# A fused long convolution and gated FFN: x rows loaded singly, index work on GpSimd, and the 1174 steps in a new order

## The chip, the cores and the metric

The kernel runs on one core of a Trainium2 chip. The metric is the device time of one execution in microseconds, the median of several runs. Engines are named as in the profile: PE (TensorE, matmuls), DVE (VectorE), ACT (ScalarE), POOL (GpSimd), and SP (SyncE), which here only issues DMAs. Each engine runs its own instructions strictly in order and waits on semaphores for the others.

## The reference

x, k and v are 2048 x 640 (S x D), all bfloat16; F is 1728. The layer norm of x feeds two branches, and the second gates the result:

```python
xn = layernorm(x)
# branch A: a 4-tap causal shift of k, times v, then a long causal convolution
kv = sum(k_pad[:, t:t+S, :] * shift_k[:, 3-t] for t in range(4)) * v
y  = irfft(rfft(kv, 2*S) * rfft(ssm_k, 2*S))[:S] + kv * ssm_D
s  = xn * y
# branch B: feed-forward
g  = silu(gelu(xn @ w1 + b1) @ w2 + b2)
out = x + s * g
```

## The kernel before

**The convolution** is done with matmuls. A transform of 4096 points is taken in two stages. Stage one multiplies with 128x128 matrices WA and WB, which are sines that the kernel makes itself from integer products of row and column numbers; stage two multiplies with 32x32 matrices `mats`, also made on the chip. Between the stages the rows have to change places, so stage one's result goes to DRAM (scrU for kv, scrK for the convolution's own kernel ssm_k) and comes back in another order. The two spectra are multiplied on DVE, taken back through 32x32 blocks (`ma`, `mb`), stored to scrC, loaded, and taken through stage one's inverse (`y`).

**Steps.** A hand-written `prologue()` opens the kernel: x chunk 0 (four rows of 128 partitions x 640) is loaded and normed, turned around on PE into xnT, and the first six blocks of the first FFN matmul are made. It also loads the small parameters: the taps skp, and b1 and ssm_D into one tile prm (`load_params`, three loads on ACT's queue), which PE turns around at L750. Then a string PLAN of 1174 steps is run in its order; each step issues one or a few instructions, and the string is the only thing that sets the order on each engine. The steps that matter below:

- `cv` (L534, L541, L545): kv on DVE, 128x1280 each: 64 steps in eight slices of eight; in each slice four products with a tap and three sums (L545, L541), and last the product with v (L534). cv31 finishes slice 3, cv63 slice 7, and `uf` 6i to 6i+5 read slice i
- `kf`, `uf` (L501): stage one for ssm_k and for kv; `ke`, `ue` move the result out of PSUM; `ks`, `us` store it (L516, L527), `fl`, `ml` load it again
- `ff`, `mu` (stage two) and `ma`, `mb` (its inverse): `blocks()`, four matmuls 32x32 (L395)
- `mp`, `mq` (L605): the products of a `mu` result in PSUM with the kernel's spectrum and its swapped copy, which `ma` and `mb` read; `me` moves their sum out of PSUM
- `h`, `he`, `g`, `ge` (L440, L447, L461, L467): FFN matmuls, gelu, FFN matmuls, silu
- `ls`, `lv`, `lr`, `ln`, `tt`, `te`: layer norm of x chunks 1 to 3 and their turning
- `w` (L299, the AND of the 128x2048 integer table) and `s` (the small matrices' integer table), which sines on ACT (`ws`, `ss`) then read

A mark .a or .d behind a step that moves data out of PSUM, or norms a row, says whether ACT or DVE does it (`evac`, L140). The block matmuls put their four 32x32 pieces at a quarter of the array that depends on the step's number:

```python
def blocks(out, m, rhs, turn, start=True, stop=True):
    for i in range(P // QB):
        j = (i + turn) % (P // QB)
        a, b = (slice(x * QB, (x + 1) * QB) for x in ((i, j) if m == F2 else (j, i)))
        nc.tensor.matmul(out=out[b, :], lhsT=mats[a, m, a], rhs=rhs[a, :], start=start, stop=stop)
```

`turn` is the step's number, P // QB is 4. The calls `ff`, `mu` of equal number modulo 4 use the same four pieces, and so do `ma` and `mb`, with the sign of the shift the other way.

Tiles, buffers and semaphores are handled by the framework. DMAs that SP and ACT issue signal one of eight completion semaphores, DMAHW0 to DMAHW7, given out in turn over the program; GpSimd's have eight of their own.

Of the kernel before, what the change touches and what calls it, by code (L numbers as in the profile page):

```python
# [28 lines left out]
WARM = (6, 3, 1)  # L29
# [3 lines left out]
w em4 em7 X1 he1 he0 he2 he3 ls6 ls7 ls5 K1 B0 h10 K0 B1 C4 he4 ls4 B2 ee7.a ee4.a he5 cv16 em6 ee6.a he10 h6 he6 lv1  # L33
lr1 ln6.a ln5.a ln4.a h13 h9 em5 he13 ee5.a h8 h11 he8 he9 s h12 he11 cv0 cv17 ln7.a cv8 he12 cv1 cv9 cv18 cv19 cv2 h7
tt8 tt9 tt7 tt6 cv20 cv10 cv11 te9.d he7 g0 g1 g2 C0 C1 C3 te6.d cv21 ws0 C2 ge0 te8.d cv22 cv3 ws1 d ge1 ge2 kt15
kc15.a kt7 cv12 te7.d kc7.d kt13 kt6 kt0 kt14 kc13.d V2 K2 kt1 kt5 kt8 kc0.d kc6.d tt5 kt2 kt11 kc14.d ws2 kc5.d V7
te5.d kc11.d kc1.a kt9 kf47 kc9.d kf46 kc8.a ke46.a kt3 kc3.a kt12 kc2.d kt4 kf28 kt10 K3 kc12.d kc4.d kc10.d cv13
gm0.d ke47.a kf40 ke40.a ke28.a kf4 kf17 kf29 kf26 kf16 ke17.a ke29.a ke26.a kf15 kf10 ke16.a ke10.a ke4.a g3 cv4 cv23
cv5 kf39 ge3 ke15.d gm1.d ke39.a kf41 kf34 kf5 ke5.a kf11 X2 kf45 kf27 kf33 ke11.a kf3 ke45.a ke3.a cv14 gm2.d cv40
gm3.d cv41 V0 X3 cv6 V1 g4 ke34.a ke33.a ke27.a ke41.a ks5 kf24 kf21 ke24.a kf14 kf44 kf42 kf7 kf43 cv42 cv15 ge4  # L40
ke44.a ke14.a ke42.a ke21.a ke7.a g5 ks1 ks9 ks13 kf12 kf8 kf25 kf20 ke43.d ls10 cv32 cv7 ge5 cv33 gm4.d kf0 ke12.a
# [46 lines left out]
def kernel(  # L88
# [139 lines left out]
    def load_x(c):  # L228
        for h in range(1 if c else 2):
            js = slice(2 * h, CH if c else 2 * h + 2)  # L230
            nc.sync.dma_start(out=xn_tiles[c][:, js, :], in_=x_v[:, c * CH:(c + 1) * CH, :][:, js, :])
# [439 lines left out]
    def prologue():  # L671
# [51 lines left out]
        for i in range(3):  # L723
            load_w1(i)
# [114 lines left out]
```

## Time and profile before

| | |
|---|---|
| median of 3 runs | 202.29 us (202.22 to 202.81) |
| profiled execution | 202.03 us, span 200.2 us |
| granted PE clock | 0.997 |
| PE, DVE, ACT, POOL busy | 95%, 86%, 77%, 22% of the span |
| data moved | 57.7 MB, mean 288 GB/s |
| first block matmul (L717) | 8.57 us |
| last kv product (cv31) ends | 84.43 us |

Times are in microseconds from the span's start. A timeline row has start, length, engine, line, operation, output and inputs, and in brackets how long the engine was idle before it and what the profile names as the end of that. A row "DVE L143 CAST ... x5" stands for five instructions in a row. ACTq and SPq are the queues that issue DMAs, PEld is the loading of PE's weights.

### The profile page before, as it was taken

The numbers are of one execution on the slowest core, as the hardware profiler recorded it, in microseconds if no ns is written. First come the engines' busy times: TensorE is split into PE (matmuls) and PEld (weight loads), VectorE is DVE, ScalarE is ACT, GpSimd is POOL, SyncE is SP. The second block draws the span as 40 slices with busy tenths as digits, with TensorE's granted clock in tenths as the row PEclk, the third lists the DMA queues.
The fourth block names the chain that finished last, engine by engine and source line by source line (L and its number), as shares of the span: only waits on it lengthen the run. The fifth ranks groups of instructions, "written<-read, shape, count | busy, mean of one in ns | idle before, by whom it ended". The sixth has DMA issues, their size and how long they took to land.

```text
span 200.2 us, 5094 instructions
## 1 busy us (share of the span) xinstructions
PE 191.1 (95%) x1934; PEld 111.4 (56%) x1934; DVE 172.8 (86%) x370; ACT 154.3 (77%) x303; POOL 45.0 (22%) x78
## 2 busy tenths in 40 slices
PE   7799999999999999999989999999999999999990
PEld 2484468866654545664645433347665454667760
DVE  7889999999999999999988999999999300199991
ACT  3469999999999999999979999984868557611030
POOL 8202000013475622153030001011055700001230
PEclk9999999999999999999999999999999999999998
DMA  6999999377699499999699999979368869991373
GB/s 196 354 394 331 361 391 411 124 263 265 184 399 419 151 328 328 363 390 384 234 276 366 337 313 315 298 271 284 92 209 291 307 185 338 395 393 52 134 273 123
DMA packets 27055, 57.69 MB, mean 288 GB/s; under 512 B 3030, under 2 KB 15511, under 8 KB 27030
## 3 DMA queue, kind: packets, MB, share of 16 engines
q1 hardware_dynamic: 22528, 39.65, 58.5%
q0 software_dynamic: 4320, 17.70, 23.5%
q8 instruction: 15, 0.25, 0.5%
q14 instruction: 10, 0.08, 0.1%
q10 hardware_dynamic: 182, 0.01, 0.1%
HBM read 33.76 MB, written 18.35 MB: 260 GB/s over the span
## 4 chain that ended last, share of the span: by engine, by line
PE 74%; ACT 8%; DVE 6%; DMA 5%; issue 2%; SPq 1%; POOL 1%; POOLq 0%; ACTq 0%; DVEq 0%
PE banks L461 25%; PE banks L440 23%; PE banks L501 8%; PE banks L395 7%; ACT area L142 4%; DMA area<-scrK 3%; PE banks L490 3%; DMA area<-scrU 2%; PE banks L650 2%; PE banks L651 2%; ACT xn L421 2%; PE banks L430 2%; DVE st L402 2%; PE banks L717 1%; ACT hT L447 1%
## 5 line engine op out<-in xcount | busy, mean ns | idle before, releaser
L142 ACT CAST area<-banks 128x426 bf16<-128x426 f32 (+2 forms) x172 | 80.0, 621 | 5.9 <-PE banks L395 4.5
L461 PE MATMUL banks<-w_sb,hT 128*128 128x320 bf16 x448 | 65.3, 299 | 0.1
L440 PE MATMUL banks<-xnT,w_sb 128*128 128x512 bf16 x250 | 58.3, 379 | 0.2
L461 PEld LDWEIGHTS <-hT 128*128 128x128 bf16 x448 | 42.8, 98 | 18.9 <-issue 2.8
L605 DVE TENSOR_TENSOR area<-banks,area 128x426 bf16<-128x426 f32 (+1 forms) x96 | 50.1, 591 | 1.3 <-PE banks L395 0.7
L447 ACT ACTIVATE hT<-banks,b_f 128x512 bf16<-128x512 f32 (+1 forms) x56 | 37.4, 715 | 5.8 <-PE banks L440 4.4
L440 PEld LDWEIGHTS <-w_sb 128*128 128x128 bf16 x250 | 23.1, 98 | 29.7 <-issue 5.2
L467 ACT ACTIVATE sl<-banks 128x320 bf16<-128x320 f32 x32 | 15.1, 486 | 19.4 <-PE banks L461 13.7
L545 DVE TENSOR_TENSOR area<-area 128x1280 bf16<-128x1280 bf16 x32 | 25.3, 813 | 0.3
L473 DVE TENSOR_TENSOR xn<-xn,sl 128x320 bf16<-128x320 bf16 x32 | 9.8, 314 | 15.5 <-ACT sl L467 15.4
L395 PE MATMUL banks<-area,mats 32*32 32x426 bf16 (+1 forms) x768 | 21.8, 345 | 0.6 <-DMA area<-scrK 0.3
L635 POOL DMA_DIRECT2D scrC<-area x16 | 11.7, 731 | 46.3 <-DMA area<-scrU 17.7
L541 DVE TENSOR_TENSOR area<-area 128x1280 bf16<-128x1280 bf16 x24 | 19.1, 817 | 0.0
L516 POOL DMA_DIRECT2D scrK<-area x16 | 8.8, 554 | 34.1 <-DMA area<-in_A_v_dram 23.8
L501 PE MATMUL banks<-area,WA 128*128 128x428 bf16 (+1 forms) x64 | 15.8, 299 | 0.0
L501 PE MATMUL banks<-area,WB 128*128 128x426 bf16 (+1 forms) x64 | 15.5, 299 | 0.0
L395 PEld LDWEIGHTS <-mats 32*32 32x32 bf16 x768 | 7.9, 88 | 12.4 <-issue 8.8
L143 DVE CAST area<-banks 128x426 bf16<-128x426 f32 (+1 forms) x24 | 13.3, 590 | 1.7 <-PE banks L395 1.7
L527 POOL DMA_DIRECT2D scrU<-area x16 | 8.7, 546 | 17.0 <-ACT area L142 17.0
L659 DVE TENSOR_TENSOR area<-banks,xn 128x426 bf16<-128x426 f32 (+1 forms) x18 | 9.7, 590 | 0.8 <-PE banks L651 0.8
L402 DVE BATCH_NORM_STATS2 st<-xn 128x6 f32<-128x320 bf16 x24 | 10.3, 472 | 0.0
L668 POOL DMA_DIRECT2D out_dram<-area x6 | 3.3, 547 | 30.7 <-DVE area L664 25.5
(99 smaller groups left out, 184.7 us busy)
## 6 DMA issues: line engine op xcount, KB each, us to landing
scrK<-area POOLq DMA_DIRECT2D x16, 320.0 KB, 5.8
area<-scrK SPq DMA_DIRECT2D x16, 320.0 KB, 5.6
scrU<-area POOLq DMA_DIRECT2D x16, 320.0 KB, 4.7
area<-area SPq DMA_DIRECT2D x32, 160.0 KB, 4.1
area<-scrU SPq DMA_DIRECT2D x16, 320.0 KB, 5.6
scrC<-area POOLq DMA_DIRECT2D x16, 320.0 KB, 3.5
area<-scrC SPq DMA_DIRECT2D x16, 320.0 KB, 6.5
area<-in_A_k_dram SPq DMA_DIRECT2D x4, 640.0 KB, 8.5
```

The lines of the kernel that those rows point to most:

```text
L142: return nc.scalar.copy(out=out_ap, in_=in_ap)
L143: return nc.vector.tensor_copy(out=out_ap, in_=in_ap)
L395: nc.tensor.matmul(out=out[b, :], lhsT=mats[a, m, a], rhs=rhs[a, :], start=start, stop=stop)
L402: nc.vector.bn_stats(out=st[:, j, h, :], in_=xn_tiles[c][:, j, h * HALF:(h + 1) * HALF])
L440: nc.tensor.matmul(out=ps, lhsT=w1_sb[:, t, ft * P:(ft + 1) * P], rhs=xnT[:, t, :], start=(t == 0), stop=(t == DT - 1))
L447: nc.scalar.activation(out=hT[0:M, ft, :], in_=one(("h", i))[0:M, :], func=ACT.Gelu_apprx_tanh, bias=b1_f[0:M, ft:ft + 1], scale=1.0)
L461: nc.tensor.matmul(out=ps[:, 0:HALF], lhsT=hT[0:M, ft, q * P:(q + 1) * P], rhs=w2_sb[0:M, ft, hs], start=(ft == 0), stop=(ft == FT - 1))
L467: nc.scalar.activation(out=sl[:], in_=one(("g", i))[:, 0:HALF], func=ACT.Silu)
L501: nc.tensor.matmul(out=ps[:, dst], lhsT=(WA, WB)[r][:, n2, :], rhs=rows[:, n2 % 2, src], start=True, stop=True)
L541: nc.vector.tensor_tensor(out=uc, in0=uc, in1=tmp, op=ALU.add)
L545: nc.vector.tensor_tensor(out=tmp if s else uc, in0=kh[:, r0:r0 + KC, :], in1=w_exp[:, j:j + 1, :].to_broadcast([P, KC, D]), op=ALU.mult)
L605: nc.vector.tensor_tensor(out=flat(("p", i))[:, x * w:x * w + w], in0=one(("mu", i))[:, 0:w], in1=flat(key)[:, cols(j)], op=ALU.mult)
```

## The change

Three things are edited.

1. **Loads.** x chunk 0 comes as row 0, row 1, w1 part 0, rows 2 and 3, w1 parts 1 and 2, where it was rows 0 and 1, rows 2 and 3, then w1.
2. **GpSimd.** The 128x2048 integer product moves from DVE (L295) to POOL (L296), behind POOL's three memsets. The small matrices' table, some eighteen DVE instructions in step `s`, is made on POOL (`small_grids`, L340 to L363); six tiny ones stay on DVE at the very start (`small_index`), and of `s` only one AND over 128x384 (L367) stays. In the opening, bn(2) moves behind the first xnT copy, two small copies move from DVE to ACT, and the second tap's copy moves behind the xnT copy. One warming matmul moves from ahead of the turned x to the start.
3. **PLAN** is written anew. `mp` and `mq` of one number stand next to each other no longer, so that other steps come between them. `w` and `s` stand at its start. The marks change too (ACT/DVE): ke 46/2 to 41/7, kc 4/12 to 7/9, ln 9/3 to 6/6, fe 36/12 to 39/9, ue 41/7 in both.

The core of the diff:

```diff
-WARM = (6, 3, 1)
+WARM = (7, 3, 0)
 PLAN = """
-w em4 em7 X1 he1 he0 he2 he3 ls6 ls7 ls5 K1 B0 h10 K0 B1 C4 he4 ls4 B2 ee7.a ee4.a he5 cv16 em6 ee6.a he10 h6 he6 lv1
+h13 w s he3 X1 em7 he1 he0 h12 he2 he4 ls7 ls4 ls6 K0 ls5 lv1 ee7.a he13 cv8 cv0 h9 em4 h11 he5 he12 cv1 lr1 B2 h10
...
-mp24 mq24 mp11 mq11 mp25 mq25 mu26 ma8 mu13 mb8 ff37 mu18 ge15 h28 he28 me8.a fe37.a h40 mp13 mq13 mp26 mq26 he40 h29
+ge14 g15 gm13.d ge15 ff34 mu13 ma8 ma6 mu25 mb8 mp25 h29 he29 mp13 mk4 mq25 mq18 me8.a h40 ml5 fl13 mu26 mk1 mq13 ma10
+mb10 mb6 ma11 mb11 mu14 mp26 fe34.a ma9 h39 he40 mp14 me6.a me11.a mq26 mq14 mu3 mb9 ff38 ff1 mu5 ff39 mp3 he39 fe38.a
...
     def load_x(c):
-        for h in range(1 if c else 2):
-            js = slice(2 * h, CH if c else 2 * h + 2)
-            nc.sync.dma_start(out=xn_tiles[c][:, js, :], in_=x_v[:, c * CH:(c + 1) * CH, :][:, js, :])
+        nc.sync.dma_start(out=xn_tiles[c][:], in_=x_v[:, c * CH:(c + 1) * CH, :])
+
+    def load_first_x(a, b):
+        nc.sync.dma_start(out=xn_tiles[0][:, a:b, :], in_=x_v[:, a:b, :])
...
-    s16 = scratch([NJ], F32)
-    r2 = scratch([P], F32)
+    s16 = scratch([NJ], I32)
+    r2 = scratch([P], I32)
...
-        nc.vector.tensor_tensor(out=prod, in0=s16[:, :, None].to_broadcast([P, NJ, P]),
+        nc.gpsimd.tensor_tensor(out=prod, in0=s16[:, :, None].to_broadcast([P, NJ, P]),
                                 in1=r2[:, None, :].to_broadcast([P, NJ, P]), op=ALU.mult)
...
+        c8 = scratch([2], F32)
+        for i in range(2):
+            nc.gpsimd.tensor_single_scalar(out=c8[:, i:i + 1], in_=c_in, scalar=8.0 * (i + 1), op=ALU.mult)
+        prod_n = scratch([P], F32)
+        nc.gpsimd.tensor_scalar(out=prod_n, in0=n_out, scalar1=n_in, scalar2=152.0, op0=ALU.mult, op1=ALU.add)
+        nc.gpsimd.tensor_tensor(out=ph[:, 0, :], in0=prod_n, in1=c_out, op=ALU.add)
+        nc.gpsimd.tensor_tensor(out=ph[:, 2, :], in0=prod_n, in1=c_out, op=ALU.subtract)
...
+        nc.gpsimd.tensor_copy(out=q, in_=ph)
         sm.update(q=q, sn=scratch([3, P], F32), mask=mask)
+
+    def small_phase():
+        nc.vector.tensor_single_scalar(out=sm["q"], in_=sm["q"], scalar=31, op=ALU.bitwise_and)
...
         make_identity(nc, ident[:])
+        small_index()
         nc.vector.memset(prm[:], 0.0)
-        load_x(0)
-        for i in range(3):
-            load_w1(i)
+        load_first_x(0, 1)
+        load_first_x(1, 2)
+        load_w1(0)
+        load_first_x(2, 4)
+        load_w1(1)
+        load_w1(2)
...
-        build_f1_product()
-        small_iotas()
         nc.gpsimd.memset(w1_sb[:, :, F:FT * P], 0.0)
         nc.gpsimd.memset(hT[FLAST:FLAST + 1, FT - 1, :], 1.0)
         nc.gpsimd.memset(kh[0:1, 0:3, :], 0.0)
+        build_f1_product()
+        small_grids()
...
-        tap_out(1)
         turn(0)
         turn(1)
-        bn(2, 0)
         turned_out("d", 0, 0)
         turned_out("a", 1, 0)
-        bn(2, 1)
-        ag(2)
-        nc.vector.tensor_copy(out=b1_f[:], in_=pt[:, 0:FT])
-        nc.vector.tensor_copy(out=dD_sb[:], in_=pt[:, FT:FT + DT])
-        bn(3, 0)
-        bn(3, 1)
-        ag(3)
+        nc.scalar.copy(out=b1_f[:], in_=pt[:, 0:FT])
+        nc.scalar.copy(out=dD_sb[:], in_=pt[:, FT:FT + DT])
+        tap_out(1)
+        for j in (2, 3):
+            bn(j, 0)
+            bn(j, 1)
+            ag(j)
```

How the compiled order moves, at three places. A row is the line, the operation, its output and inputs, and the semaphores it waits on.

SP's queue at the very start, before (in_A_q is x, in_B_w is w1 or w2, in_A_k is k):

```order
L231 DMA xn<-in_A_q_dram 128x1280 x2
L257 DMA w_sb<-in_B_w_dram 128x5x384 x2
L257 DMA w_sb<-in_B_w_dram 128x5x960 [waits DMAHW0_49]
L231 DMA xn<-in_A_q_dram 128x2560 [waits DMAHW1_49]
L238 DMA area<-in_A_k_dram 128x2560 [waits DMAHW2_49]
L264 DMA w_sb<-in_B_w_dram 128x5x640 [waits DMAHW3_49]
```

and now:

```order
L232 DMA xn<-in_A_q_dram 128x640 x2
L258 DMA w_sb<-in_B_w_dram 128x5x384
L232 DMA xn<-in_A_q_dram 128x1280
L258 DMA w_sb<-in_B_w_dram 128x5x384
L258 DMA w_sb<-in_B_w_dram 128x5x960
L229 DMA xn<-in_A_q_dram 128x2560
L237 DMA area<-in_A_k_dram 112x1920 [waits DMAHW2_49]
```

Seven loads stand ahead of the first wait where four did, and x chunk 1 has come ahead of k; the seven take the semaphores 1 to 7.

ACT at the same place, before (skp is the taps' tile, its load, ACT's first, takes semaphore 0; prm is the parameters' tile; skT and area are the taps turned around and spread out):

```order
L249 DMA prm<-in_B_b_dram 13x128
L251 DMA prm<-in_B_b_dram 1x64
L253 DMA prm<-in_A_ssm_D_dram 5x128
L744 COPY skT<-banks 4x640 [waits PE_49]
L685 ACTIVATE sd<-mv,eps 128x2 [waits DVE_49,Activation_49]
```

and now:

```order
L250 DMA prm<-in_B_b_dram 13x128 [waits DMAHW0_49]
L252 DMA prm<-in_B_b_dram 1x64 [waits DMAHW1_49]
L254 DMA prm<-in_A_ssm_D_dram 5x128 [waits DMAHW3_49]
L748 COPY skT<-banks 4x640 [waits PE_49]
L685 ACTIVATE sd<-mv,eps 128x2 [waits DVE_49,Activation_49]
```

The three loads now each wait for an earlier load to land: for skp, for x row 0, for w1 part 0. On PE, the turning of prm (L750 before, L754 now) stands ahead of the turning of x (L708) in both.

DVE where the prologue ends, before (xnT is the turned x, area<-area 128x2048 the AND of the large table, st and mv the statistics of chunk 1):

```order
L143 COPY xnT<-banks 128x3x256 [waits PE_49]
L299 TENSOR_SCALAR area<-area 128x2048
L402 BN_STATS st_274<-xn 128x6 [waits DMAHW1_49]
L402 BN_STATS st_274<-xn 128x6
L403 BN_AGGR mv_275<-st_274 128x2 [waits DVE_49]
```

and now:

```order
L143 COPY xnT<-banks 128x3x256 [waits PE_49]
L300 TENSOR_SCALAR area<-area 128x2048 [waits Pool_49]
L367 TENSOR_SCALAR area<-area 128x384 [waits Pool_49]
L402 BN_STATS st_304<-xn 128x6 [waits DMAHW7_49]
L402 BN_STATS st_304<-xn 128x6
L403 BN_AGGR mv_305<-st_304 128x2 [waits DVE_49]
```

Both ANDs now wait for POOL, and the statistics stand behind the second one.

More of the change, by code (lines that the diff above doesn't have):

```diff
@@ L37 @@
[L37 to L41, printed above, removed]
@@ new lines @@
+fe45.a fe29.a cv55 cv29 cv63 g8 cv30 fe15.a ge8 uf39 ue39.a fe3.a ln8.d uf41 g9 uf47 ue41.a fe6.d cv31 uf40 ue47.a ge9
+ue40.d uf32 uf43 ue32.d uf45 uf38 ue45.a fl0 uf22 uf20 ue22.a ue20.a ue43.d ue38.d ff31 uf44 ue44.a us9 fe31.a uf42
+ue42.d uf19 uf18 ff16 ue18.a ue19.a us10 fe16.d fl7 uf46 tt10 tt12 uf23 ff8 ue23.a te10.d uf36 uf21 ue46.d fe8.a
+ue36.a us8 ue21.d uf37 ff7 ff17 fe17.a fe7.a ff47 ff25 ff26 it2 ff21 te12.d fe47.d fe26.d fe25.a ue37.a fe21.a ff23
+ff11 gm9.d ls13 ff9 ff0 ff22 fe22.a fe11.a fe0.a g10 us14 us15 us6 us13 us7 us12 fe9.a ff32 gm7.d ie2.d gm8.d fe23.d
```

134 lines of the change are left out of this document (61 added, 73 removed).

## The prediction

> **What bounds the kernel now.** I read the page first, then the busy time by stage, then the timeline where PE waits, then the opening. Page, busy time and count of PE:
>
> ```profile
> PE 191.1 (95%) x1934; PEld 111.4 (56%) x1934; DVE 172.8 (86%) x370; ACT 154.3 (77%) x303; POOL 45.0 (22%) x78
> ```
>
> PE is busy 95% of the span, so the average says that PE is the bound. The stages say more (start and end, length, busy time of each engine, PE clock, DMA share, GB/s):
>
> ```profile
> 12.40:84.50 72.10, 71.59 (x512) 44.60 (x510) 71.31 (x144) 69.83 (x136) 18.25 (x29) 1.00 0.87 310
> 84.50:111.00 26.50, 25.75 (x371) 14.73 (x370) 25.02 (x59) 25.00 (x55) 6.40 (x12) 1.00 0.94 333
> 111.00:157.00 46.00, 45.99 (x743) 22.63 (x742) 44.41 (x92) 38.03 (x78) 9.63 (x14) 1.00 0.82 266
> ```
>
> From 12.4 to 84.5 DVE is as full as PE, 71.3 of 72.1 us. Which of the two waits, the timeline shows at the end of that stretch (start, length, engine, line):
>
> ```profile
> 81.17 0.79 DVE L423 TENSOR_SCALAR xn<-xn,mv,rs 128x640 bf16<-128x640 bf16 x2
> 81.89 0.81 DVE L534 TENSOR_TENSOR area<-area 128x1280 bf16<-128x1280 bf16 x1
> 82.76 0.27 PE L501 MATMUL banks<-area,WA 128*128 128x212 bf16 x1
> 83.66 0.77 DVE L534 TENSOR_TENSOR area<-area 128x1280 bf16<-128x1280 bf16 x1
> ...
> 85.45 2.63 DVE L143 CAST area<-banks 128x426 bf16<-128x426 f32 x5
> 85.58 0.34 PE L501 MATMUL banks<-area,WA 128*128 128x428 bf16 x1
> ...
> 189.77 5.06 PE L461 MATMUL banks<-w_sb,hT 128*128 128x320 bf16 x36
> ```
>
> L534 at 81.89 is step cv63, the product that finishes kv slice 7; it ends at 82.70, and the transform uf43 that reads it starts at 82.76: PE waits for DVE here. L534 at 83.66 is cv31, the last product with v of all, ending at 84.43; uf21, its first reader, runs from 85.58 to 85.92. Behind it nothing on PE waits for kv work, and PE ends its last matmul at 194.83. So there are two legs: DVE from its early table work to cv31, then PE to the end.
>
> **The opening.** Waits of SP's queue, the landing line of the x loads (L231), that of the last stores (L485), and the timeline:
>
> ```profile
> SPq L257 <- DMA skp<-in_A_shift_k_dram: 1.4, 1, 1.4
> SPq L264 <- DMA w_sb<-in_B_w_dram: 0.7, 1, 0.7
> ...
> DMA to landing us min/median/max: 3.1/3.6/8.3
> ...
> DMA to landing us min/median/max: 2.1/2.1/2.1
> ...
> 0.72 0.85 SPq L231 DMA_DIRECT2D xn<-in_A_q_dram  x2
> 2.12 0.36 ACTq L253 DMA_DIRECT2D prm<-in_A_ssm_D_dram  x1
> 6.32 0.38 SPq L264 DMA_DIRECT2D w_sb<-in_B_w_dram  x1
> 6.62 0.09 PEld L750 LDWEIGHTS <-prm 19*128 19x128 bf16 x1 [0.75 <-DVE rstd L688]
> 7.13 0.81 PE L708 MATMUL banks<-ident,xn 128*128 128x128 bf16 x10
> 7.87 0.56 DVE L143 COPY xnT<-banks 128x768 bf16<-128x768 bf16 x1
> 8.57 2.89 PE L717 MATMUL banks<-xnT,w_sb 128*128 128x256 bf16 x25 [0.63 <-ACT xnT L142]
> 9.09 0.88 DVE L679 BATCH_NORM_STATS2 stats<-xn 128x6 f32<-128x320 bf16 x2
> 10.24 0.29 ACT L685 ACTIVATE sd<-mv,eps 128x2 f32<-128x2 f32 x1 [1.68 <-DVE mv L682]
> 12.48 1.22 DVE L299 TENSOR_SCALAR area<-area 128x2048 int32<-128x2048 int32 x1
> ```
>
> The first two rows are queue waits for a load that has nothing to do with the load being issued. A DMA takes the next of eight completion semaphores in turn, and one that reuses a semaphore is held, with everything behind it on its queue, until the earlier load has landed. L264 is issued at 6.32 because w1_0 has landed.
>
> The new opening sends seven loads from SP where there were four ahead of the first wait, so the three tiny loads of prm on ACT's queue now get used semaphores: skp's, x row 0's, w1_0's. The last is the late one. Before, the second x load was the one ahead of w1_0; it started some 0.43 us after 0.72 and took about 3.6, landing near 4.8, so w1_0 came 1.5 us behind the x bytes ahead of it. Now x rows 0 and 1 (the bytes of the first x load) are ahead, landing near 3.85, so w1_0 lands near 5.35 and the last prm load is issued then instead of at 2.12. How long will it take? Lower bound 2.1 us (L485, an emptying queue); upper bound, as measured loads go, 4.5, since L750 reads prm at 6.62, 4.5 after L253's issue, among the same traffic. I take 4.0, nearer to the same load: prm lands at 9.35.
>
> [...]
>
> On PE, L750 stands ahead of the turns of x (L708). From a landing at 9.35: L750, then L708 at 9.65, first copy of xnT 0.74 later (7.87 against 7.13) at 10.4, first_block 1.44 later (8.57 against 7.13) at 11.1, +2.5. On DVE both bn(2) and bn(3) now stand behind that copy: the copy (0.47 until the next starts), then twice 1.15 (9.09 to 10.24: L679 twice and its L682), so L685 at 13.15; from L685 to L299 it was 2.24 (10.24 to 12.48), so the AND of the table, L299 before and L300 now, starts at 15.4, not 12.48: **+2.9**. The 2.29 us of L295 that leave DVE earn nothing, for they ran while DVE had no x row.
>
> **GpSimd.** Two groups by line (busy us, mean ns), then GpSimd's timeline:
>
> ```profile
> L295 DVE TENSOR_TENSOR area<-area 128x2048 int32<-128x2048 f32 x1 | 2.3, 2292 | 0.6 <-POOL area L294 0.6
> L414 POOL TENSOR_SCALAR nb<-nb 128x4 f32<-128x4 f32 x3 | 1.1, 380 | 0.3
> ...
> 1.64 1.90 POOL L329 IOTA area<- 128x128 f32 x3
> 3.47 0.38 POOL L737 MEMSET w_sb<- 128x320 bf16 x1
> 4.48 1.69 POOL L739 MEMSET area<- 1x1920 bf16 x1
> ```
>
> The small iotas were done by 1.64, the three memsets took 3.47 to 6.17. Memsets first, the product can start near 4.35. Its price over 2048 elements a partition: below, 1.8 us by L739 (0.88 ns an element, which only writes); above, 8.4, by L329 (0.63 us for 128, 4.1 ns an element with 0.1 us taken off for the start). I take 4.0, about twice L739's, since it reads as well. Then the three iotas 1.9, two tiny steps 0.6, nine of 128x128 at 0.38 to 0.66 (L414, L329), taken 0.45, 4.05, and one cast of three such, 0.75: the chain ends at **15.7** (13.4 to 20.1 at the product's bounds). DVE's 128x384 AND (L367), just behind the table's, waits for it, and behind L367 stand the statistics of chunk 1 and every kv product. DVE reaches it at 15.4 + 1.2 = 16.6, so GpSimd is covered by 0.9, and the cover goes if prm is quick. [...]
>
> **DVE from the AND to cv31.** First and next step after the small phase, then two groups:
>
> ```profile
> 18.39 0.14 DVE L339 TENSOR_SCALAR area<-area 128x1 int32<-128x1 int32 x1
> 21.82 1.55 DVE L545 TENSOR_TENSOR area<-area 128x1280 bf16<-128x1280 bf16 x2
> ...
> L143 DVE COPY area<-banks 128x640 bf16<-128x640 bf16 x12 | 4.9, 477 | 0.0
> L402 DVE BATCH_NORM_STATS2 st<-xn 128x6 f32<-128x320 bf16 x24 | 10.3, 472 | 0.0
> ```
>
> It took 12.48 to 84.43, 71.95. The small phase shrinks from 3.43 to 0.3: -3.1. But the new plan, by its .a and .d marks ahead of cv31, gives DVE six more evacuations ke and fe (0.53 each, 2.63 for five): +3.2; four more ln (0.36, 81.17 to 81.89 for two): +1.4; two fewer copies of 477 ns net: -0.9; one fewer ls: -1.1. Net -0.5. So cv31 ends at 15.4 + 71.95 - 0.5 = 86.85, **+2.4**.
>
> **PE from cv31's reader to the end.** Runs of 32x32 block matmuls (L395) between ffn1 groups:
>
> ```profile
> 119.35 0.56 PE L395 MATMUL banks<-area,mats 32*32 32x426 bf16 x24
> 119.85 1.25 PE L440 MATMUL banks<-xnT,w_sb 128*128 128x512 bf16 x5
> 121.03 0.73 PE L395 MATMUL banks<-area,mats 32*32 32x426 bf16 x28
> 121.70 1.25 PE L440 MATMUL banks<-xnT,w_sb 128*128 128x512 bf16 x5
> ...
> 124.79 0.57 PE L395 MATMUL banks<-area,mats 32*32 32x426 bf16 x28
> 125.29 1.25 PE L440 MATMUL banks<-xnT,w_sb 128*128 128x512 bf16 x5
> ```
>
> From start to start, 24 matmuls hold PE for 0.50 us, 28 for 0.67, and 28 others for 0.50 again: what counts is not their number. By the plan's step numbers it is how often the same quarter of the array comes up, that is how many steps of a run share their number modulo 4 (negated for ma and mb), at 0.17 a time. Undone pairs mp, mq leave new runs such as "mu26 ma10 mb10 mb6 ma11 mb11 mu14 ma9", five deep. Counted so over both plans behind the first reader of cv31: 73 layers in 31 runs before, 81 in 29 now: +8 x 0.17, and -2 x 0.25 for two runs fewer, +0.85. One more g falls on this side (14 matmuls of L461, 5.06 x 14/36): +1.95. Two fewer uf, 0.2 each (the 0.27 of one matmul at 82.76 overlaps the next): -0.4. Together **+2.4**. Before, this leg took 194.83 - 85.92 = 108.9, in which PE idled 0.75 (84.5 to 111.0, row above). I take off all of that, for the kernel's half of the transform now has 2.4 us more until its readers: a choice, kept open down to nothing. uf21 also started 1.15 behind cv31; the new plan's first reader, uf22, I let start at once, at 86.85, and end at 87.2. PE ends at 87.2 + 108.9 + 2.4 - 0.75 = 197.75, +2.9. The tail behind the last matmul is the same instructions.
>
> **Sum.** The profiled execution took 202.03 (span 200.2), the median is 202.29, 0.26 more. 202.03 + 2.9 + 0.26 = **205.2**.
>
> **Rivals.** (a) prm lands at 7.45 (the 2.1 us row). The AND starts at 13.5, DVE reaches L367 at 14.7 and waits there for GpSimd until 15.7: it keeps 0.9 of the 1.9 gained. 204.3. For it: the load is some hundred bytes on a queue of its own. (b) The prm load waits for all that SP has queued by then, 2.7 MB at some 330 GB/s, and lands near 13: the AND starts at 19, 3.6 later, **208.8**. Against it: L253 did not. (c) GpSimd's product takes 8.4 us and DVE stands at L367 until 20.1, 3.5 longer: 208.7. (d) The other side: the last prm load is no brake. It lands by 6.6, when L750 wanted it before; the AND starts at 12.65, GpSimd is done by 13.9, and DVE spends none of the 0.8 us that it idled of 72.1. Then cv31 ends at 12.65 + 71.95 - 0.5 - 0.8 = 83.3, uf22 at 83.65, PE at 83.65 + 108.9 + 2.4 - 0.75 = 194.2, 0.6 earlier: 201.65; with layers that cost nothing 200.8. It decides once the AND starts before 12.7. For it: 2.29 us and 3.1 us really leave DVE. Against it: the waits stand in the compiled order, and it would have to land 1.25 us after its issue, and the quickest landing above is 2.1. (e) Gains and losses cancel, within 0.3%.
>
> **How the numbers follow.** A measurement of this kernel tells 0.3%, 0.6 us, from no change. Forecast 0.40; (a) 0.22; (b) 0.14; (c) 0.06; (d) 0.13; (e) 0.05. Slower 0.82. The range runs from 202.4, which leaves out (d) and part of (e), to 208.5, short of (b) and (c) as priced though not of milder forms of them; between lie 0 to 0.75 us of PE idling, the 1.15 behind cv31, and prm landings from 7.45 to 12.5.
>
> **What would show it.** Right: the last prm load issued near 5.4, L754 near 9.4, first L717 near 11.1, L300 near 15.4, L367 without a wait, last kv product near 86.9, last matmul near 197.7. Wrong: prm issued by 3, L717 before 9, or L367 idle for GpSimd; or PE idle ahead of its late uf steps gone, which would mean that DVE no longer binds.

## The result: 210.7 us against 202.4, and outside the range

The changed kernel takes 210.71 us (median of four runs, 209.03 to 212.89), the kernel before 202.39 beside it: a ratio of 1.038, interval 1.031 to 1.045. Slower was forecast, but 205.2, and the range ended at 208.5. The profiled execution is the quickest of the four, 209.03 us with a span of 207.2; what follows explains its 7.0 us over the profiled 202.03 of before. The other 1.7 us to the median lie in runs without a trace. Here and below a ratio compares undisturbed runs only, while a median is over all runs.

PE's busy time on the page of the changed kernel:

```profile
PE 193.8 (94%) x1934; PEld 114.2 (55%) x1934; DVE 171.1 (83%) x358; ACT 155.8 (75%) x305; POOL 58.9 (28%) x91
```

PE is as busy as before to within 3 us, DVE has 1.7 us less, GpSimd 14 us more. The opening: the waits that stood out, two pieces of the chain that ended last (start, length), then the timeline:

```profile
ACT skT L748 <- DMA w_sb<-in_B_w_dram: 3.9, 1, 3.9
PE banks L754 <- DMA prm<-in_A_ssm_D_dram: 3.1, 1, 3.1
...
1.64 4.62 DMA w_sb<-in_B_w_dram
6.28 4.75 DMA prm<-in_A_ssm_D_dram
...
4.40 3.61 POOL L296 TENSOR_TENSOR area<-area 128x2048 int32<-128x2048 int32 x1
6.28 0.26 ACTq L254 DMA_DIRECT2D prm<-in_A_ssm_D_dram  x1
7.70 1.33 DVE L691 TENSOR_SCALAR xn<-xn,mv,rstd 128x640 bf16<-128x640 bf16 x2
11.16 0.17 PE L754 MATMUL banks<-ident,prm 19*128 19x19 bf16 x1 [3.15 <-DMA prm<-in_A_ssm_D_dram]
11.27 1.25 PE L708 MATMUL banks<-ident,xn 128*128 128x128 bf16 x10
12.34 0.56 DVE L143 COPY xnT<-banks 128x768 bf16<-128x768 bf16 x1 [3.31 <-PE banks L708]
12.95 4.37 PE L717 MATMUL banks<-xnT,w_sb 128*128 128x256 bf16 x25 [0.44 <-DVE xnT L143]
16.03 0.62 POOL L363 CAST area<-area 128x384 int32<-128x384 f32 x1
17.80 0.56 DVE L143 COPY xnT<-banks 128x768 bf16<-128x768 bf16 x1 [1.51 <-PE banks L708]
18.27 1.22 DVE L300 TENSOR_SCALAR area<-area 128x2048 int32<-128x2048 int32 x1
19.41 0.35 DVE L367 TENSOR_SCALAR area<-area 128x384 int32<-128x384 int32 x1
```

The chain is the forecast one: the last prm load is held until w1's first part has landed, PE stands at the turning of prm, x is turned late, the AND of the table comes late, and L367 behind it does not wait for GpSimd, done at 16.65. But every link is longer, and there is one that the prediction did not have. Busy times and clock of the changed kernel between 9 and 17 us (the clock is the third number from the end):

```profile
9.00:11.00 2.00, 0.00 (x0) 0.00 (x0) 0.03 (x1) 0.00 (x0) 1.68 (x6) 0.54 1.09 375
11.00:13.00 2.00, 1.40 (x12) 1.14 (x13) 0.66 (x2) 0.45 (x1) 1.81 (x4) 0.50 1.04 364
13.00:15.00 2.00, 2.00 (x10) 1.44 (x11) 1.85 (x6) 0.92 (x5) 1.84 (x4) 0.50 1.06 248
15.00:17.00 2.00, 2.00 (x16) 1.59 (x14) 0.97 (x3) 1.74 (x3) 1.65 (x3) 0.76 0.98 339
```

While PE waits its granted clock falls to half, at about 9.2, and comes back only at 16.0: the first 25 block matmuls take 4.37 us where they took 2.89, and the second turn of x stands behind them.

From the AND to the last product with v (L534), and from there to PE's last matmul:

```profile
18.27:91.99 73.72, 71.63 (x519) 44.70 (x517) 71.27 (x132) 69.60 (x137) 23.01 (x30) 1.00 0.85 309
91.99:202.25 110.26, 109.99 (x1347) 62.20 (x1346) 90.70 (x194) 79.26 (x156) 20.66 (x33) 1.00 0.75 261
...
91.18 0.81 DVE L534 TENSOR_TENSOR area<-area 128x1280 bf16<-128x1280 bf16 x1
195.82 6.43 PE L461 MATMUL banks<-w_sb,hT 128*128 128x320 bf16 x46
```

In the kernel before these two legs are 71.95 and 110.40 us. So the AND starts 5.8 us later than before, DVE's leg is 1.8 longer, PE's leg 0.1 shorter; PE ends 7.4 us later and the tail behind it is 0.4 shorter: 7.0.

### The profile page after: what moved, and what is told of

It reads as the page before. It is cut to its first block, busy times and chain, and to the rows that moved or that the text cites. A ratio compares the mean times of both kernels' runs of the same rounds, so it can differ in the third digit from the quotient of the medians.

```text
span 207.2 us, 5105 instructions
## 1 busy us (share of the span) xinstructions
PE 193.8 (94%) x1934; PEld 114.2 (55%) x1934; DVE 171.1 (83%) x358; ACT 155.8 (75%) x305; POOL 58.9 (28%) x91
## 4 chain that ended last, share of the span: by engine, by line
PE 55%; DVE 20%; ACT 11%; DMA 5%; POOL 4%; issue 2%; SPq 0%; DVEq 0%; ACTq 0%
PE banks L461 21%; PE banks L440 14%; PE banks L395 9%; ACT area L142 8%; DVE area L545 6%; DVE area L541 4%; POOL rs L411 4%; DMA prm<-in_A_ssm_D_dram 2%; DVE area L143 2%; DMA w_sb<-in_B_w_dram 2%; PE banks L650 2%; PE banks L717 2%; PE banks L651 2%; ACT hT L447 2%; DVE st L402 1%
## 5 line engine op out<-in xcount | busy, mean ns | idle before, releaser
L142 ACT CAST area<-banks 128x426 bf16<-128x426 f32 (+2 forms) x169 | 77.0, 563 | 8.2 <-PE banks L395 7.4
L461 PE MATMUL banks<-w_sb,hT 128*128 128x320 bf16 x448 | 65.3, 299 | 0.2
L461 PEld LDWEIGHTS <-hT 128*128 128x128 bf16 x448 | 42.7, 98 | 19.5 <-issue 3.1
L447 ACT ACTIVATE hT<-banks,b_f 128x512 bf16<-128x512 f32 (+1 forms) x56 | 36.5, 702 | 5.8 <-PE banks L440 3.1
L467 ACT ACTIVATE sl<-banks 128x320 bf16<-128x320 f32 x32 | 14.3, 460 | 17.8 <-PE banks L461 17.0
L545 DVE TENSOR_TENSOR area<-area 128x1280 bf16<-128x1280 bf16 x32 | 25.0, 818 | 1.2 <-ACT area L142 1.0
L395 PE MATMUL banks<-area,mats 32*32 32x426 bf16 (+1 forms) x768 | 22.2, 344 | 0.2
L501 PE MATMUL banks<-area,WA 128*128 128x212 bf16 (+1 forms) x64 | 15.9, 299 | 0.9 <-DVE area L534 0.9
L395 PEld LDWEIGHTS <-mats 32*32 32x32 bf16 x768 | 9.5, 88 | 12.2 <-issue 9.8
L501 PE MATMUL banks<-area,WB 128*128 128x214 bf16 (+1 forms) x64 | 16.1, 299 | 0.0
L143 DVE CAST area<-banks 128x426 bf16<-128x426 f32 (+2 forms) x27 | 14.8, 582 | 1.4 <-PE banks L395 1.3
L411 POOL TENSOR_TENSOR rs<-ve,mhalf 128x4 f32<-128x4 f32 x3 | 8.5, 2840 | 18.4 <-DVE ve L407 18.4
```

The source lines that it names most:

```text
L142: return nc.scalar.copy(out=out_ap, in_=in_ap)
L143: return nc.vector.tensor_copy(out=out_ap, in_=in_ap)
L411: nc.gpsimd.tensor_tensor(out=rstd[:], in0=live["ve", c][:], in1=mhalf[:, 0:CH], op=ALU.pow)
L447: nc.scalar.activation(out=hT[0:M, ft, :], in_=one(("h", i))[0:M, :], func=ACT.Gelu_apprx_tanh, bias=b1_f[0:M, ft:ft + 1], scale=1.0)
L461: nc.tensor.matmul(out=ps[:, 0:HALF], lhsT=hT[0:M, ft, q * P:(q + 1) * P], rhs=w2_sb[0:M, ft, hs], start=(ft == 0), stop=(ft == FT - 1))
L467: nc.scalar.activation(out=sl[:], in_=one(("g", i))[:, 0:HALF], func=ACT.Silu)
```

## The experiments

Theory after the result: the late AND makes the loss, nearly one for one, because the stretch behind it is full, and the new order adds to it. Rival: the new order of steps alone makes the loss, and the opening is hidden. The first four kernels part these. Each ratio is against the kernel before, run beside it; that kernel's median lay between 202.4 and 204.0 us from one group of runs to the next, so across groups the ratios say more than the times.

**The prm loads written early.** The loads of skp and prm move ahead of w1's second part, and prm's memset ahead of the six tiny index steps:

```diff
+        nc.vector.memset(prm[:], 0.0)
         small_index()
-        nc.vector.memset(prm[:], 0.0)
...
+        for i in range(3):
+            load_params(i)
         load_w1(1)
         load_w1(2)
...
         nc.vector.memset(eps[:], LN_EPS)
         nc.scalar.activation(out=sd[:, 0:1], in_=eps[:], func=ACT.Sqrt)
-        for i in range(3):
-            load_params(i)
```

> The changed kernel with the three small prm loads issued ahead of the second and third part of w1, so that none of them reuses a completion semaphore. Theory (the opening): in the changed kernel the last prm load is issued at 6.28 and lands at 11.1, PE stands idle 3.1 us, its granted clock falls to 0.5, and the AND of the table (L300) starts at 18.27. Here prm should land near 6.5, the clock should stay at 1.0, L300 should start near 13 to 13.5, and then L367 has to wait for GpSimd, whose chain ended at 16.65 in the changed kernel: L367 near 16.7 instead of 19.41, 2.7 us earlier, total near 208.0 us against 210.7. Rival (the new order of steps costs the time): no more than 1 us gained, 209.7 to 210.7.

208.58 us, ratio 1.024 (1.017 to 1.031). Timeline:

```profile
4.40 3.61 POOL L296 TENSOR_TENSOR area<-area 128x2048 int32<-128x2048 int32 x1
6.29 2.74 DVE L691 TENSOR_SCALAR xn<-xn,mv,rstd 128x640 bf16<-128x640 bf16 x2
7.96 1.89 POOL L340 IOTA area<- 128x128 f32 x3
8.24 0.28 PEld L708 LDWEIGHTS <-xn 128*128 128x128 bf16 x5 [1.61 <-DVE xn L691]
14.57 2.47 POOL L360 TENSOR_SCALAR area<-area 128x128 f32<-128x128 f32 x2
15.24 1.22 DVE L300 TENSOR_SCALAR area<-area 128x2048 int32<-128x2048 int32 x1
16.99 0.50 POOL L363 CAST area<-area 128x384 int32<-128x384 f32 x1
17.53 0.36 DVE L367 TENSOR_SCALAR area<-area 128x384 int32<-128x384 int32 x1 [1.08 <-POOL area L363]
```

prm is there in time, the AND is 3.0 us earlier than in the changed kernel, and three things take its place. DVE's two norms, 0.80 us before, take 2.74: the first 1.90, until just behind the end of GpSimd's product (8.01), the second 0.84 beside GpSimd's iotas. The clock, which was to stay at 1.0, is 0.57 from 9 to 13 us. And L367 waits 1.08 for GpSimd, partly for a delay that the AND itself makes: of GpSimd's two steps L360 the first takes 0.73 us, the second, which falls beside the AND, 1.76, and it ends 0.6 behind the AND. 2 to 3 us are gained (2.1 by the medians, 2.9 by the ratios, whose intervals touch), where 2.7 was expected, though L300 is 2 us later than expected.

**The opening alone** (the changed kernel with the old PLAN) and **the order alone** (the kernel before with the new PLAN):

```diff
 PLAN = """
-h13 w s he3 X1 em7 he1 he0 h12 he2 he4 ls7 ls4 ls6 K0 ls5 lv1 ee7.a he13 cv8 cv0 h9 em4 h11 he5 he12 cv1 lr1 B2 h10
+w em4 em7 X1 he1 he0 he2 he3 ls6 ls7 ls5 K1 B0 h10 K0 B1 C4 he4 ls4 B2 ee7.a ee4.a he5 cv16 em6 ee6.a he10 h6 he6 lv1
```

and the rest of the string with it; in the second kernel the other way round.

> The changed kernel with the PLAN string of before: its opening alone. Theory (the opening costs most): L300 at 18.3 as in the changed kernel, 5.8 us later than before, less the 3.1 us of the small phase that left DVE behind it: between 205 and 208.5 us, taken 207. Rival (the new order): the opening is hidden, 202.4 to 203.5 us.

> The kernel before with the PLAN string of the change: the new order alone, with the small phase back on DVE. Theory (the opening): L299 at 12.5; DVE's leg to cv31 then takes the 73.7 us of the changed kernel plus the 3.1 of the small phase, cv31 ends near 89.3, 4.9 later than before, of which 1.2 is slack, and the leg behind it takes 1.0 more: near 207 us, or 204 if DVE's idle time in the changed kernel came from its opening. Rival (the new order costs the time by itself): 209 us or more. A third view (the new order is good and only its opening is bad): 201 to 202.5 us.

The opening alone: 210.08, ratio 1.030 (1.023 to 1.037). The order alone: 207.52, ratio 1.018 (1.012 to 1.024). Each part alone is slower; the opening alone loses as much as the whole change, within the intervals. Its AND stands at 19.67, not 18.3: in this profile of the same opening w1's first part landed 1 us later. The legs from the AND to the last L534, in this order: before, opening alone, order alone:

```profile
12.48:84.43 71.95, 71.44 (x510) 44.49 (x508) 71.16 (x144) 69.68 (x136) 18.25 (x29) 1.00 0.87 310
...
19.67:91.94 72.27, 71.03 (x510) 44.44 (x508) 68.66 (x127) 69.51 (x136) 19.05 (x29) 1.00 0.78 279
...
12.55:89.46 76.91, 73.38 (x519) 45.23 (x517) 74.25 (x149) 69.61 (x137) 22.90 (x30) 0.98 0.88 313
```

With the old plan DVE has 2.5 us less to do and the leg is not shorter: PE is busy 71.0 of its 72.3 us. With the new plan and all its own work DVE is busy 74.25 us and the leg takes 76.9. What the leg hangs on shows in the chain that ended last. By engine, of the kernel before and of the changed kernel:

```profile
PE 74%; ACT 8%; DVE 6%; DMA 5%; issue 2%; SPq 1%; POOL 1%; POOLq 0%; ACTq 0%; DVEq 0%
...
PE 55%; DVE 20%; ACT 11%; DMA 5%; POOL 4%; issue 2%; SPq 0%; DVEq 0%; ACTq 0%
```

Within the leg alone the chain of the kernel before runs through PE for some 52 of the 72 us and through DVE for 6; that of the opening alone, with the same plan, for 48 and 5; that of the changed kernel through DVE for 39 of the 73.7, ACT 21, GpSimd 9 and PE 1.5. So DVE, with ACT, binds in the new plan, and PE in the old one, where moving 3.1 us of small-matrix work to GpSimd is worth nothing. In the new plan the leg is 3.2 us shorter with that work gone (76.9 to 73.7); that the work alone makes the 3.2 is not shown, since the two kernels differ in their whole opening and the order alone had a clock of 0.93 from 30 to 50 us.

**Clock kept up by more warming matmuls.** In the changed kernel, seven ahead of the turning of prm:

```diff
+        warm(7)
         pt = banks[:, 5, :].bitcast(BF16)
```

> The changed kernel with seven more warming matmuls (0.43 us each) on PE between the taps and the turning of prm, where PE stood idle from 8.0 to 11.1. Theory (idle time drops the clock): the granted clock stays at 1.0 from 9 to 17 us (0.50 to 0.76 in the changed kernel), the first 25 block matmuls take 2.9 us instead of 4.37, the first turn 0.8 instead of 1.25, L300 starts near 17.0 instead of 18.27: 209.4 us against 210.7. Rival (the clock costs nothing, since DVE and not PE sets the end): within 0.3 us of the changed kernel.

211.08, ratio 1.035 (1.028 to 1.042). The clock stays at 1.0 in the profiled execution and the 25 matmuls take 2.90 us, as expected, but in this profile w1's first part landed 0.6 us later, prm's turning came at 12.16 instead of 11.16, and L300 stands at 18.22. From prm's turning to L300 it is 6.06 us against 7.11: the clock took 1.05 of that link. On the total this run decides nothing. It was tried again without the load, below.

**The product back on DVE** (in the kernel with prm early; the call also moves ahead of GpSimd's memsets, and its index rows are fp32 again):

```diff
-        nc.gpsimd.tensor_tensor(out=prod, in0=s16[:, :, None].to_broadcast([P, NJ, P]),
+        nc.vector.tensor_tensor(out=prod, in0=s16[:, :, None].to_broadcast([P, NJ, P]),
```

> The kernel with the prm loads early, and the 128x2048 product back on DVE, where it stands in the kernel before (0.7 us later, behind the six tiny steps). With the product on GpSimd the first norm (L691) took 1.90 us instead of 0.44 and ended when the product ended. Theory (GpSimd's long instruction holds up DVE): both L691 of the first pair take 0.44 to 0.55, the first block matmul starts near 9.3 instead of 10.3, L300 near 13.5 instead of 15.2, GpSimd's table is done near 13.5 and L367 hardly waits: L367 near 14.7 instead of 17.5, 205.8 us against 208.6. Rival (the slow norm comes from something else, the clock or the DMAs): L691 stays over 1 us, and the total within 0.7 us of 208.6.

206.34, ratio 1.014 (1.006 to 1.021).

```profile
7.18 0.89 DVE L691 TENSOR_SCALAR xn<-xn,mv,rstd 128x640 bf16<-128x640 bf16 x2
13.40 1.22 DVE L300 TENSOR_SCALAR area<-area 128x2048 int32<-128x2048 int32 x1
14.54 0.35 DVE L367 TENSOR_SCALAR area<-area 128x384 int32<-128x384 int32 x1
```

The norms take 0.89 us, L300 starts 1.8 earlier, L367 no longer waits and is 3.0 earlier: the theory's places within 0.2 us, its total within 0.6. Not all of the 1.8 is GpSimd's: in this profile the clock stayed at 1.0 from 9 to 13 us, with prm early alone it was 0.57. The last run below has the product on GpSimd at full clock and L300 at 14.34, so that some 0.9 is the product's.

**prm early, with the old plan:** the two edits above together, the early loads and the old PLAN.

> The kernel with the prm loads early and the PLAN string of before. In the run with the changed opening and the old plan, DVE took 72.3 us from the AND of the table to cv31 though 3.1 us of work had left it, because PE and ACT are as full there. Theory (the relief of DVE earns nothing in this stretch; what is left is the late opening): L300 near 15.2 as with the new plan, cv31 near 87.3, 2.9 later than before: 205.3 us. Rival (DVE alone is the bound, and the relief counts): cv31 near 84.2, 202 to 202.5 us.

206.39, ratio 1.015 (1.006 to 1.024). L300 at 15.24, the last L534 ends at 86.74: a leg of 71.5, with 68.8 us of DVE work. The relief again earns nothing. The total is 1 us above what was expected.

**New order, old marks.** Each step keeps its new place, but ACT or DVE as in the old plan; a line of it:

```diff
-ln6.a he11 ee4.a he9 he10 K1 B0 B1 cv9 cv2 ln7.d cv16 cv17 cv10 ln4.d h7 ln5.a he7 h8 em5 cv18 h6 tt5 tt6 tt7 em6 he8
+ln6.a he11 ee4.a he9 he10 K1 B0 B1 cv9 cv2 ln7.a cv16 cv17 cv10 ln4.a h7 ln5.a he7 h8 em5 cv18 h6 tt5 tt6 tt7 em6 he8
```

> The kernel with the old opening and the new order of steps, but each step that moves data out of PSUM or norms a row on the engine (ACT or DVE) that the old plan gave it. Theory (the new marks load DVE with 2.6 us more ahead of cv31, and DVE binds there): cv31 at 86.0 to 87.5 instead of 89.5, total 204.5 to 206 against 207.5. Rival (ACT is as full and takes the time instead, or the order itself costs it): 207 us or more.

219.50, ratio 1.078 (1.072 to 1.083): the theory's gain did not come, and the rival was too mild. DVE's waits and the leg:

```profile
DVE area L545 <- ACT area L142: 3.4, 1, 3.4
DVE xn L473 <- ACT sl L467: 2.6, 1, 2.6
...
12.49:93.60 81.11, 73.40 (x513) 44.76 (x511) 73.26 (x145) 70.55 (x137) 21.06 (x30) 0.98 0.84 299
```

DVE has 1 us less work than with the new marks and the leg is 4.2 longer: it stands behind ACT, for 6.0 us in these two waits. That is 4 of the 12 us by which the kernel is slower than the order alone; 7 more lie behind cv31 (118.9 against 111.6 us to PE's last matmul) and are not explained here. The marks belong to their order; the count of DVE's work alone does not give the leg.

**The small table alone on GpSimd,** in the kernel before:

```diff
-        small_iotas()
...
         turned_out("a", 1, 0)
+        small_index()
+        small_grids()
         bn(2, 1)
```

> The kernel before with one part of the change: the small matrices' table on GpSimd (six tiny steps stay on DVE, in the opening behind the first copy of xnT; GpSimd's part starts at about 8.8 and is done before step s). Loads, product and plan are those of before. Theory (PE and ACT are as full as DVE from 12 to 84 us, 71.6 and 69.8 of 72.1): the 2.2 us net that leave DVE earn under 0.5 us; the opening may lose up to 0.8: within 0.8 us of before. Rival (DVE alone binds): 2 us faster than before.

203.78 against 203.20, ratio 1.002 (0.997 to 1.007): no change, as the theory has it. Its profile, of an execution of 208.68 us, is not used.

**Why prm waits.** Two memsets of DVE go ahead of the six tiny index steps, in the changed kernel:

```diff
-        small_index()
+        nc.vector.memset(eps[:], LN_EPS)
         nc.vector.memset(prm[:], 0.0)
+        small_index()
...
-        nc.vector.memset(eps[:], LN_EPS)
```

> The changed kernel with two DVE memsets (eps and prm) ahead of the six tiny index steps instead of behind them; nothing else moves. In the compiled order the three prm loads then come before the second and third part of w1 in the giving out of completion semaphores and wait for no load. Theory (the six tiny steps, which wait for GpSimd's first iota, delayed the prm loads in that order, and this alone made them wait): prm in time for 6.7, L300 near 15.2, total near 208.5 as with the loads written early, 2 us under the changed kernel. Rival (the seven loads ahead of the first wait are to blame, as the prediction had it): 210 us or more.

208.47, ratio 1.025 (1.018 to 1.032). prm's turning starts at 6.46, and w1's later parts wait for semaphores in its stead. The theory holds: with the memsets ahead of the six steps the prm loads wait for no load, with the same loads from SP. The steps wait for GpSimd's first iota, the memsets stood behind them, ACT's first instructions behind these, and so the completion semaphores were given to SP's loads first; of this chain only the first link was varied. The loads do not bring the wait by themselves. **The loads alone,** in the kernel before, say the same:

```diff
-        load_x(0)
-        for i in range(3):
-            load_w1(i)
+        load_first_x(0, 1)
+        load_first_x(1, 2)
+        load_w1(0)
+        load_first_x(2, 4)
+        load_w1(1)
+        load_w1(2)
```

> The kernel before with one part of the change: x row 0, row 1, w1 part 0, rows 2 and 3, w1 parts 1 and 2. In its compiled order the prm loads wait for no load. Theory: nothing waits for the second x row, since DVE is at its product until 3.93, so L299 near 12.5 and within 0.6 us of before. Rival (x rows earlier start everything earlier): up to 0.7 us faster; rival of the prediction (the new order of loads brings the wait): 4 us slower.

205.01 against 203.13, ratio 1.004 (0.999 to 1.009): no change can be told. prm's turning starts at 6.25, so the prediction's rival falls. In the profile the AND is late all the same (14.68, where 12.5 was expected), since bn(2) stands ahead of the first xnT copy there and its rows now come behind w1, and PE's clock was at 0.58 from 9 to 13 us. The leg from the AND to the last L534 (14.68 to 86.63) is 71.95 again.

**The two waits of DVE in the new plan** (in the kernel with the product on DVE). From the changed kernel:

```profile
73.96 5.93 POOL L411 TENSOR_TENSOR rs<-ve,mhalf 128x4 f32<-128x4 f32 x1 [2.51 <-DVE ve L407]
79.92 0.45 DVE L423 TENSOR_SCALAR xn<-xn,mv,rs 128x640 bf16<-128x640 bf16 x1 [0.95 <-POOL rs L411]
...
32.33 2.29 DVE L545 TENSOR_TENSOR area<-area 128x1280 bf16<-128x1280 bf16 x3 [1.03 <-ACT area L142]
```

In the plan two pairs move up, lv2 and lr2, em5 and ee5 (only the steps around them are shown):

```diff
-h21 lv2 uf2
+h21 uf2
-cv39 cv58 lr2 h22
+cv39 cv58 h22
-ke14.a ls10 gm4.d
+ke14.a ls10 lv2 lr2 gm4.d
-ln5.a he7 h8 em5 cv18
+ln5.a em5 ee5.a he7 h8 cv18
-he8 ee5.a cv3
+he8 cv3
```

> The kernel with prm early and the product on DVE, and two moves in the new plan: lv2 and lr2 (the power on GpSimd, 5.93 us beside DVE's back-to-back products, for which DVE waited 0.95) directly behind the statistics they need, and em5, ee5 (the tap for which DVE waited 1.0) ahead of he7. Theory (these two waits are what makes DVE's stretch from L300 to cv31 longer than DVE's work): the stretch takes 72.0 instead of 73.9, cv31 near 85.4, total near 204.6 against 206.3. Rival (PE and ACT are as full, and the waits only show it): the stretch stays over 73.3, within 0.7 us of 206.3.

208.51, ratio 1.028 (1.020 to 1.036): both waits are gone, the power takes 1.05 us at its new place instead of 5.93, and the kernel is 2 us slower. The leg is 75.0 against 73.9, with a new wait, 2.6 us of L545 for a store to scrU, and the AND comes 1.3 us later (14.73), the clock having fallen to 0.59 from 9 to 13 us. The expected 72.0 did not come: taking these two waits away does not shorten the leg, since another comes in their place.

**Product first on GpSimd,** with prm early and the old plan:

```diff
+        build_f1_product()
         nc.gpsimd.memset(w1_sb[:, :, F:FT * P], 0.0)
         nc.gpsimd.memset(hT[FLAST:FLAST + 1, FT - 1, :], 1.0)
         nc.gpsimd.memset(kh[0:1, 0:3, :], 0.0)
-        build_f1_product()
```

> The changed opening without its waits, with the old plan: prm loads early, and GpSimd's product ahead of its memsets (1.65 to 5.3), so that it is done before the first norms. Theory (GpSimd's product holds up the norms only while it runs): L691 takes 0.44 to 0.55 each, L300 near 12.5 to 12.8 as in the kernel before, and as the stretch to cv31 gains nothing from the relief of DVE, 202.5 to 204 us, within 0.7 us of before. Rival: the relief of DVE shows now that the opening is in time, 200 to 201.5 us. Rival: the memsets on GpSimd hold up the norms as well, 204.5 us or more.

206.53, ratio 1.016 (1.009 to 1.023): the third case came.

```profile
1.77 3.61 POOL L296 TENSOR_TENSOR area<-area 128x2048 int32<-128x2048 int32 x1
6.29 2.74 DVE L691 TENSOR_SCALAR xn<-xn,mv,rstd 128x640 bf16<-128x640 bf16 x2
6.31 1.69 POOL L742 MEMSET area<- 1x1920 bf16 x1
```

Now it is the memset, ending at 8.00, that holds up the first norm just as long (1.90 us); that product and memset end at the same time is chance. Beside an idle GpSimd, in the kernel before, L691 took 0.80 us for two; beside the product (with prm early) and beside the memset (here) it took 2.74. How a GpSimd instruction holds up a norm is not shown. L300 stands at 16.70 here, with the clock at half from 8.7 to 15.5, so the norms are not all that separates this kernel from the one before.

**Warming, once more.** More warming matmuls in the kernel before, between the turns and the first blocks:

```diff
         tap_out(1)
+        warm(1, 4)
         turn(0)
         turn(1)
+        warm(2, 4)
```

> The kernel before with two more warming matmuls, between the turns of the first x rows and the first block matmuls, into a bank that is free then (one of them takes 0.22 us at full clock). Runs of kernels with this opening ranged from 202.2 to 206 us on one chip, and profiles show the granted clock from 9 to 13 us either at 1.0 or near 0.58. Theory (the fall of the clock in the opening spreads the runs): the runs lie closer, 202.0 to 203.2, median near 202.3, 0.3 to 0.6% under the kernel before. Rival (the spread comes from elsewhere, the landing of the loads): median and spread as before, within 0.3%.

203.43 against 203.69, ratio 1.002 (0.998 to 1.007). The rival holds: the runs in the ratio still lie between 202.35 and 204.53 (201.54 to 204.17 in the kernel before), and they do not go with the clock: those with a mean granted clock of 0.999 took 202.43 to 204.16, those with 0.992 took 202.47 to 204.53. Where the spread comes from is open. The same in the kernel with the two memsets first, `warm(6, 4)` ahead of the turns and `warm(2, 4)` behind:

> The changed kernel with the two memsets first, so that prm waits for no load, and eight warming matmuls in the two pauses of PE ahead of the first block matmuls (6.8 to 8.3 and 9.5 to 10.3 in the run without them, whose clock was 0.50 to 0.65 from 9 to 17 us). Theory (the clock is worth what the block matmuls ahead of the second turn take longer): 25 block matmuls take 2.9 us instead of 5.5, L300 near 15.0 instead of 16.8, but L367 then waits for GpSimd until 16.5 instead of 18.0: 207.1 us against 208.5. Rival (DVE and GpSimd set the end of the opening): within 0.5 us of 208.5.

208.53, ratio 1.030 (1.025 to 1.035), against 1.025 without the warming: no gain.

```profile
10.17 2.89 PE L717 MATMUL banks<-xnT,w_sb 128*128 128x256 bf16 x25 [0.20 <-ACT xnT L142]
14.34 1.25 DVE L300 TENSOR_SCALAR area<-area 128x2048 int32<-128x2048 int32 x1
14.59 2.29 POOL L360 TENSOR_SCALAR area<-area 128x128 f32<-128x128 f32 x2
17.37 0.36 DVE L367 TENSOR_SCALAR area<-area 128x384 int32<-128x384 int32 x1 [1.79 <-POOL area L363]
```

L300 is 2.5 us earlier than without the warming (16.82), and L367 only 0.6 (17.37 against 17.96): the clock's price is hidden behind GpSimd's table. The table itself ends 0.8 us later than without the warming (17.33 against 16.50), because the early AND now falls on L360, which takes 2.29 us for two instead of 1.44. With prm in time and the clock up, GpSimd sets the end of the opening.

No version of these beats the kernel before.

## Where the prediction was right and where it failed

Two steps of the sum failed: the AND's late start was sized at +2.9 us and came at +5.8, and DVE's leg to cv31 was to shrink by 0.5 us and grew by 1.8. That the kernel is slower was forecast rightly, and for the most part for the right reason.

**The mechanism of the opening was right, each of its terms too small.** The last prm load was issued at 6.28, not 5.35: w1_0 took 4.6 us from its issue at 1.64, as long as before, so the step that let it land 1.5 us behind the x bytes failed; fewer bytes ahead of it did not bring it earlier. The load then took some 4.8 us, over the bound of 4.5, not 4.0. These two make 1.7 of the 2.9 us by which the AND missed its 15.4. Most of the remaining 1.2 is the clock: from prm's turning to L300 it took 7.11 us with the clock at half, 6.06 with more warming, about what the prediction had for it. The prediction priced PE's pause as time, not as what it does to the clock. In the changed kernel's trace the clock was 0.65 from 9.0 to 9.5 us and 0.50 behind, so that it fell at 9.2, when PE had stood idle for 1.1 us; it was full again at 16.0, 4.8 us after PE's work began anew at 11.2. What sets these two times is not shown.

**Its reason for the wait was wrong.** Seven loads from SP where there were four were said to make the prm loads reuse semaphores; the runs with the memsets first and with the loads alone show that these loads bring no wait where the six tiny DVE steps do not stand ahead of the two memsets. Whether the old loads would wait behind the six steps was not run.

**GpSimd.** 3.61 us for the product, against 4.0, and 16.65 for the end of the table, against 15.7, without a wait of L367, as forecast. The last is partly luck: at the forecast 16.6 DVE would have reached L367 just when the table ended, and it was the AND's further delay that covered it. Rival (a) was the right picture of what comes next: with prm in time, the new plan and the product on GpSimd, L367 stands at 17.4 to 18.0, and waits 1.1 and 1.8 us for GpSimd in two of three runs; in the third (memsets first) the half clock had made the AND late enough. What no part of the prediction had is how DVE and GpSimd hold each other up: with prm early, DVE's first norm took 1.90 us beside GpSimd's product where it took 0.44 before, and a GpSimd step L360 took 1.76 beside DVE's AND where the other took 0.73. In the changed kernel the norms lost 0.5 us by it, hidden behind the wait for prm.

**DVE's leg.** The term "-0.5" should have been +1.8. The work itself came near: DVE was busy 71.27 us against 71.16, where -0.5 was forecast. But DVE idled 2.45 us of the leg against 0.8, and the forecast carried the old 0.8 over. Two of these waits are seen, 1.0 and 0.95; taking them away brought others, so the cause of the longer leg is open beyond this. That the small phase's 3.1 us would count in full fits the new plan (3.2) and is wrong in the old (nothing).

The picture behind this term was read wrongly from the kernel before. "PE waits for DVE here", at 82.76, does not hold: PE was at block matmuls until then,

```profile
82.22 0.54 PE L395 MATMUL banks<-area,mats 32*32 32x428 bf16 x8
```

and the only wait of PE that the profile names from the AND to cv31 is 0.3 us, for ACT. In the kernel before PE sets this stretch; it is the new plan that hands it to DVE and ACT. There PE does wait for cv31, by 0.28 us at 92.04.

**PE's leg.** cv31's end to PE's last matmul: 110.9 was forecast, 110.26 measured, 110.40 before. PE was busy 0.35 us more in it than before and idle 0.5 less. The block matmuls (L395) took 21.62 us against 21.24, +0.38 where their depth was priced at +0.85, with 12 fewer of them on this side, and L461 44.93 against 43.44, +1.5 where +1.95 was forecast. That the depth of a run is what costs was not tested.

Added up in the profiled execution: 2.9 for the AND, 2.3 for DVE's leg, -0.65 for PE's leg, -0.4 for the tail, 4.1 us in all, which is 209.03 less the 204.95 forecast for it.

## What to carry to other kernels

When a change moves work in the opening, look in the compiled order at what each small load now waits for, and price a pause of PE twice, as time (3.1 us ahead of prm's turning in the changed kernel) and as the clock behind it (1.05 us from there to the AND). Work moved to GpSimd was not free beside DVE's norms and ANDs (1.90 us for a norm of 0.44, 1.76 for a GpSimd step of 0.73): look up what DVE runs beside its long instructions. DVE's statistics kept their 0.83 us for two there. Taking work off an engine pays only where the chain that ends last runs through it: 3.1 us off DVE were worth nothing in the order of steps where the chain ran through PE, and went with a leg 3.2 us shorter in the one where it ran through DVE. How full the engines are did not tell these two apart.

## What the runs showed of the hardware

- A DVE `tensor_scalar` of 0.44 us on bfloat16 took 1.90 us (prm early) to 2.15 (memsets first with warming) beside GpSimd's product, and 1.90 beside a memset that writes one partition alone (product first). BATCH_NORM_STATS2 took 0.83 us for two beside the same product (changed kernel, at 4.11) and 0.83 to 0.89 in the kernel before.
- The other way round, a GpSimd `tensor_scalar` over 128x128 of 0.73 us took 1.58 us (memsets first with warming) to 1.76 (prm early) where DVE's AND over 128x2048 (1.22 to 1.25 us) ran, and ended some 0.6 us behind it.
- GpSimd's power over 128x4 took 5.93 us in the changed kernel, ending 0.9 us behind a row of DVE's products, and 1.05 at its new place in the kernel with two pairs moved up, where DVE's products ran beside it too (60.2 to 61.7 us). What makes the difference is not shown.
- A fallen clock stayed at half for 3.4, 6.8 or 10.2 us, worked out from the mean clock of stretches with 1.00 and 0.50 as its only levels: 3.4 with prm early (0.57 from 9 to 13 us, 1.00 on both sides), 6.8 in the changed kernel (9.2 to 16.0), 10.2 in the opening alone (7.7 to 17.9: 0.84, 0.50, 0.50 and 0.88 in the four stretches of 4 us from 5 on).
- PE's busy share does not by itself tell whether the clock falls: two kernels with the same opening (product on DVE, and with two pairs moved up), PE busy 3.37 and 3.04 of the 4 us from 5 to 9, were granted 1.00 and 0.59 in the next four, and the changed kernel with seven more warming matmuls, busy 2.63 of these 4 us and all of the next, kept 1.00.
